# In the second batch the products with v come one step later, each behind the scores of four steps on

## The chip, the cores and the metric

One core of a Trainium2 chip runs the whole program. The metric is the device time of one execution in microseconds, the median of several runs. The engines of the core work in parallel, each through its own queue in order: TensorE (PE, matmuls and the transposes made as matmuls), VectorE (DVE), ScalarE (ACT), GpSimd (POOL) and SyncE (SP), which here issues nearly all DMAs.

## What is computed

Attention in which a query only sees the keys of its own hash bucket, and behind it two MLPs with a gate. Cut to what matters:

```python
q_bits = (einsum('bhsd,dk->bhsk', q, proj) > 0)          # 6 bits, k_bits likewise
mask   = q_bucket[:, :, :, None] == k_bucket[:, :, None, :]
scores = where(mask, q @ k.T / sqrt(64), -1e9)
attn   = exp(scores - max);  attn /= attn.sum(-1) + 1e-9
x = (attn @ v)                                            # 2 batches, 8 heads, 768 x 64
x = x as 1536 tokens x 512
x = gate(x @ w_in,  1.702) @ w_out                        # 512 -> 2048 -> 512
y = gate(x @ w_in2, 1.0)   @ w_out2
```

## The kernel before, in words

**Steps.** A step j is one block of 128 query rows of one head: 16 heads of 6 blocks make 96 steps, 0 to 47 the first batch, 48 to 95 the second. Heads are worked on in pairs. For each step the kernel runs this chain:

- `scores` (L417, L418): four matmuls of 384 columns, two with `aq` and `ak` (q and k split into two parts), two with `BQ` and `BK`, which hold the rows of the mask and the other half of the split. I call the four S j.
- `top` on VectorE (L425) reads the scores from PSUM into `p` and takes the row's extreme; `exps` on ScalarE (L430) is the exponential; `p_high` (L441, ScalarE) rounds to f16 and `p_low` on GpSimd (L445) gives the rest. Both land in `hl`.
- `p_turn` (L451) turns `hl` into `pt` by a DMA transpose from SyncE's queue, one for two steps, j even and j+1. I call such two steps a pair and name it by the even one.
- `av` (L463 to L465): eighteen small matmuls, `pt` times the split v (`VS`). I call them av j. `norm` divides by the row sums when a head is complete.

The mask rows of a pair of heads come from `bits` (L345, matmuls into `psbit`), `signs` (L352, VectorE, `mk`) and `rows` (L360, four DMAs on SyncE's queue: `BK` and `BQ` of the one head, then of the other).

**Beside it.** From step 51 on, the first MLP for the tokens of the first batch is mixed in: `gemm1` (L632, `psh`, twelve matmuls per unit, here h) and `gemm2` (L666, `pso`, six per unit, here o), both with three products of split operands. Its weights come as 64-bit words (`raw`, L139, 512 KB each), are rebuilt on VectorE and ScalarE (L173 to L181), and the split parts are written to DRAM (`spih`, `spil`, `spoh`, `spol`, L186) and read again later (L163). When attention is done, the rest of this MLP and the second one follow; that half is matmuls almost without a break.

**PSUM and buffers.** From step 51 on the scores have one PSUM tile, the products with v one bank, the MLP two, transposes and bits two. `pt` has two buffers.

**What sets the order.** The code is written step by step (L583 to L612): in a turn i it emits av i - LAG, then `top`, the preparation of later heads, `exps`, `p_high`, `p_low`, `p_turn`, some units of the MLP, and in the second batch the scores of i + 1. With LAG = 3, av follows the exponential by three turns. A scheduler then orders each engine's instructions by when it believes them ready and by the priorities in `SOONER`; `issue_after` pins one instruction behind another. So the code's order is not the engine's order.

Of the kernel before, what the change touches and what calls it, by code (L numbers as in the profile page):

```python
# [21 lines left out]
def tile_lsh_attention_two_mlps(  # L22
# [13 lines left out]
    V, A, G, T, SP = nc.vector, nc.scalar, nc.gpsimd, nc.tensor, nc.sync  # L36

    B, H, S, D = q.shape
# [4 lines left out]
    NC = S // P  # L43
    HS = S // 2
    HC = NC // 2
    HEADS = B * H
# [13 lines left out]
    QSCALE = -1.0 / math.sqrt(D)  # L60
    assert math.frexp(QSCALE)[0] == -0.5
    NBUF = 3
    LAG = 3
    TUL = 1
    MORE = {'aq': 1, 'ak': 1, 'p': 1, 'hl': 1, 'pt': 0, 'nk': 1, 'nq': 1, 'nv': 1}
    PTB = 2
# [12 lines left out]

    SOONER = ({'ahead': 100, 'move': 20, 'load_v': 400, 'evict': 200, 'p_high': 200, 'natural': 800, 'p_turn': 35, 'turn': 100, 'p_low': 75, 'top': 35, 'exps': 75, 'bits': 300, 'norm': 35, 'load': 50, 'signs': 20}, {'scores': 200, 'evict': 50, 'norm': 300, 'av': 400, 'natural': 200, 'gate': 50, 'p_turn': 20, 'load_v': 200, 'load': 20, 'sum': 150, 'move': 20, 'p_high': 150, 'rows': 100, 'p_low': 75, 'bits': 100, 'exps': 20}, {'gate': 300, 'sum': 10, 'weights': 50})  # L80
    RATE = (3.4, 2.85)
    SWITCH = HEADS // 2 * NC + LAG + 1
    RING = 3
    RING2 = 6

# [2 lines left out]
    def sooner(task):  # L88
        n = SOONER[stage[0]].get(task, 0)
        return tc.high_priority(offset=n) if n else nullcontext()  # L90
# [161 lines left out]
    def attention(sp, s1, ps_m, ps_v, ahead_of, setup):  # L252
        nat, st = {}, {}
# [12 lines left out]
        N = len(steps)  # L266
# [65 lines left out]
        def place(n):  # L332
            return n % (NBUF + 1) if n < H else (n - H) % NBUF
# [74 lines left out]
        def scores(j):  # L408
            n, c = steps[j]
            aq, ak = st["q", n], st["k", n]  # L410
            bq, bk = BQ[place(n)], BK[place(n)]
            ps = ahead_of["pool"].tile([P, 2, 512], F32, tag="s", name="pss")
            lq = aq.rearrange("p a b -> p (a b)")[:, c * P:(c + 1) * P]
            bq = bq[:, c * P:(c + 1) * P]
            for half in range(2):
                o = ps[:, half, 0:HS]
                T.matmul(o, lhsT=lq, rhs=ak[:, half, :], start=True, stop=False)  # L417
                T.matmul(o, lhsT=bq, rhs=bk[:, half * HS:(half + 1) * HS], start=False, stop=True)  # L418
            st["S", j] = ps[:, :, 0:HS]


# [32 lines left out]
        def av(j):  # L454
            (n, c), g = steps[j], group[j]
            vs, s = st["v", n // 2]
            pt = st.pop(("pt", j))
            if j == g[0]:
                st["av", g] = v_bank("pav")
            o = st["av", g][:, c * (D + 1):(c + 1) * (D + 1)]  # L460
            for i in range(NC):
                hv, lv = vs[:, n % 2, i, 0:D + 1], vs[:, n % 2, i, D + 1:]
                T.matmul(o, lhsT=pt[:, i], rhs=hv, start=(i == 0), stop=False)  # L463
                T.matmul(o[:, 0:D], lhsT=pt[:, i], rhs=lv, start=False, stop=False)  # L464
                T.matmul(o, lhsT=pt[:, NC + i], rhs=hv, start=False, stop=(i == NC - 1))  # L465


        def norm(g):
# [35 lines left out]
        def v_bank(name):  # L504
            j = count["av"] = (count.get("av", -1) + 1) % len(ps_v)
            return ps_v[j].tile([P, 512], F32, tag="av", name=name)
# [31 lines left out]
        def run(fs):  # L538
            for f, *a in fs:
                with sooner(f.__name__):  # L540
                    f(*a)
# [38 lines left out]
            run(ahead(1, s))  # L580


        for lead, first, last in ((2, 0, N // 2), (1, N // 2, N)):  # L583
            def at(f, j):
                if first <= j < last:
                    with sooner(f.__name__):
                        f(j)

            for i in range(first - lead, last + LAG + 1):
                if lead == 2:  # L590
                    at(scores, i + 2)
                at(av, i - LAG)
                at(top, i + lead - 1)
                m = i - LAG
                if first <= m < last and m == group[m][-1]:
                    with sooner("norm"):
                        norm(group[m])
                m = i - 2 * (2 - lead)
                if first <= m < last:
                    pr, s = divmod(m, 2 * NC)  # L600
                    with sooner("ahead"):
                        if pr + 1 < HEADS // 2:
                            run(ahead(pr + 1, s))
                        if s >= 2 * NC - 4 and pr + 2 < HEADS // 2:
                            run(ahead(pr + 2, s - 2 * NC))
                at(exps, i)
                at(p_high, i)
                at(p_low, i)
                at(p_turn, i - TUL)
                yield i  # L610
                if lead == 1:
                    at(scores, i + 1)  # L612
# [108 lines left out]
    with ExitStack() as es:  # L721
# [10 lines left out]
        for i in attention(sp, s1, ps_m, ps_v, ahead_of, lambda: attention_setup(sp, s1, am, ps_m)):  # L732
# [3 lines left out]
            if gen is None and i >= WSTART and i % WEVERY == 0 and W.done < 4:  # L736
                W.step()
            if gen is None and i == SWITCH - 1:
                ps_s.close()
# [57 lines left out]
```

## Time and profile before

| | us |
|---|---|
| median of 3 runs | 806.49 |
| lowest, highest run | 803.45, 806.79 |
| the profiled execution | 809.91 |
| its span in the trace | 807.9 |
| TensorE busy in the span | 740.4 (92%) |
| VectorE, ScalarE, GpSimd busy | 507.3, 422.4, 430.4 |

The span is what the trace covers; the profiled execution's own time is 2.0 us longer. All times of the trace count from the start of its span. The second batch's scores begin at 151 us (S48) and end at 381 us (S95); the last product with v ends at 394 us. A product's wait is shown on its first matmul, in brackets, with what released it.

### The profile page before, as it was taken

To read this page: it belongs to the slowest core of one execution; us is meant where nothing else is said; L and a number is where in the kernel's file an instruction comes from. 1 tells how busy PE (TensorE), PEld (TensorE's weight loads), DVE (VectorE), ACT (ScalarE), POOL (GpSimd) and SP (SyncE) were. 2 spreads that over 40 slices of the span, in tenths; PEclk is the share of its full clock that TensorE was granted. 3 is DMA by queue.
4 is the path that set the end of the run, shared out by engine and by line. 5 is a ranking of instruction groups with operands and counts; after the bars stand their busy time and mean duration, and the time that the engine had idled before them with its cause. 6 is when DMAs were issued, how large, how long until landed. Compare 5 with 4: busy or idle time off the path is not lost.

```text
span 807.9 us, 14034 instructions
## 1 busy us (share of the span) xinstructions
PE 740.4 (92%) x5384; PEld 682.6 (84%) x5384; DVE 507.3 (63%) x932; ACT 422.4 (52%) x721; POOL 430.4 (53%) x345
## 2 busy tenths in 40 slices
PE   6786777678889999899999999979999999999998
PEld 5676666668878898899899999978998899989996
DVE  8987688967689798887332244999545744322222
ACT  6776576586778586676444134445545333311220
POOL 5675567877659666766633133567535334422220
PEclk9898888799999999999999999999999999999999
DMA  5999999999999998885597040333211300000112
GB/s 160 206 191 186 185 204 208 211 247 249 272 225 252 255 227 239 220 188 106 149 387 246 2 157 1 130 108 101 80 52 53 105 1 2 0 1 1 40 40 78
DMA packets 196270, 116.40 MB, mean 144 GB/s; under 512 B 153318, under 2 KB 175846, under 8 KB 196204
## 3 DMA queue, kind: packets, MB, share of 16 engines
q1 hardware_dynamic: 196044, 115.52, 57.5%
q8 instruction: 42, 0.69, 0.3%
q14 instruction: 24, 0.20, 0.1%
q10 hardware_dynamic: 160, 0.00, 0.0%
HBM read 56.63 MB, written 16.78 MB: 91 GB/s over the span
## 4 chain that ended last, share of the span: by engine, by line
PE 66%; DMA 13%; DVE 10%; issue 4%; ACT 3%; POOL 2%; SPq 0%; ACTq 0%; DVEq 0%; POOLq 0%
PE pso L666 29%; PE psh L632 28%; DMA pt<-hl 9%; PE pss L417 2%; PE psbit L345 2%; POOL hl L445 2%; DMA raw<-in_moe_w_in_dram 2%; DVE p L425 2%; PE pss L418 2%; DVE f L176 1%; ACT p L430 1%; PE pav L463 1%; PE pav L464 1%; PE pav L465 1%; DVE f L175 1%
## 5 line engine op out<-in xcount | busy, mean ns | idle before, releaser
L643 POOL TENSOR_TENSOR gl<-g,gh 128x384 fp32r<-128x384 f32 x128 | 136.0, 1064 | 195.7 <-ACT gh L642 183.6
L445 POOL TENSOR_TENSOR hl<-p,hl 128x768 f16<-128x768 f32 x96 | 162.6, 1700 | 71.9 <-ACT hl L441 37.4
L632 PE MATMUL psh<-XH,wih 128*128 128x384 f32 x512 | 174.2, 340 | 1.5 <-DVE part L675 1.0
L632 PE MATMUL psh<-XL,wih 128*128 128x384 f32 x512 | 172.9, 338 | 1.8 <-DVE XL L498 1.8
L632 PE MATMUL psh<-XH,wil 128*128 128x384 f32 x512 | 173.2, 338 | 0.0
L675 DVE SCALAR_TENSOR_TENSOR part<-pso,part 128x384 f32<-128x384 f32 (+1 forms) x124 | 72.6, 591 | 88.8 <-PE pso L666 88.6
L641 DVE TENSOR_TENSOR g<-g,psh 128x384 f32<-128x384 f32 x96 | 52.8, 551 | 117.5 <-ACT g L640 117.5
L430 ACT ACTIVATE p<-p,lo 128x768 f32<-128x768 f32 x96 | 89.7, 936 | 52.7 <-DVE p L425 52.2
L642 ACT CAST gh<-g 128x384 fp32r<-128x384 f32 x128 | 65.5, 513 | 78.7 <-DVE g L641 69.1
L425 DVE TENSOR_SCALAR_CACHE_REDUCE p<-pss 128x768 f32<-128x768 f32 x96 | 90.8, 948 | 15.3 <-PE pss L418 13.3
L632 PEld LDWEIGHTS psh<-XH,wih 128*128 128x128 f32 x512 | 97.5, 190 | 3.1 <-ACT XH L677 1.0
L632 PEld LDWEIGHTS psh<-XL,wih 128*128 128x128 f32 x512 | 97.6, 191 | 2.8 <-DVE XL L498 2.2
L632 PEld LDWEIGHTS psh<-XH,wil 128*128 128x128 f32 x512 | 97.3, 190 | 0.2 <-POOL wil L181 0.2
L640 ACT ACTIVATE g<-psh 128x384 f32<-128x384 f32 x96 | 46.8, 489 | 96.1 <-PE psh L632 95.2
L463 PE MATMUL pav<-VS,pt 128*128 128x65 f16 x576 | 64.4, 198 | 33.9 <-DMA pt<-hl 32.1
L666 PE MATMUL pso<-gh,woh 128*128 128x384 f32 x256 | 87.3, 347 | 6.5 <-ACT gh L642 4.3
L463 PEld LDWEIGHTS <-pt 128*128 128x128 f16 x576 | 54.6, 99 | 44.1 <-DMA pt<-hl 38.9
L666 PE MATMUL pso<-gh,wol 128*128 128x384 f32 x256 | 86.2, 337 | 0.0
L666 PE MATMUL pso<-gl,woh 128*128 128x384 f32 x256 | 86.1, 336 | 0.0
L417 PE MATMUL pss<-ak,aq 128*128 128x384 f32 x192 | 76.0, 397 | 10.8 <-DVE p L425 10.5
L666 PE MATMUL pso<-woh,gh 128*128 128x512 f32 x192 | 74.8, 390 | 0.2 <-ACT gh L642 0.2
L666 PE MATMUL pso<-wol,gh 128*128 128x512 f32 x192 | 75.0, 391 | 0.0
(119 smaller groups left out, 1572.0 us busy)
## 6 DMA issues: line engine op xcount, KB each, us to landing
raw<-in_moe_w_in_dram SPq DMA_DIRECT2D x32, 512.0 KB
raw<-in_moe_w_out_dram SPq DMA_DIRECT2D x32, 512.0 KB
spih<-wih SPq DMA_DIRECT2D x13, 256.0 KB
spil<-wil SPq DMA_DIRECT2D x13, 256.0 KB
spoh<-woh SPq DMA_DIRECT2D x13, 256.0 KB
spol<-wol SPq DMA_DIRECT2D x13, 256.0 KB
wih<-spih SPq DMA_DIRECT2D x13, 256.0 KB
wil<-spil SPq DMA_DIRECT2D x13, 256.0 KB
```

The costliest lines, as they stand in the source:

```text
L417: T.matmul(o, lhsT=lq, rhs=ak[:, half, :], start=True, stop=False)
L425: V.tensor_scalar(p, st.pop(("S", j)), LOW, None, op0=ALU.min, op1=ALU.min, accum_out=lo)
L430: A.activation(p, p, AF.Exp, bias=lo, scale=-1.0)
L445: G.tensor_tensor(out=hl[:, 1], in0=st.pop(("p", j))[0], in1=hl[:, 0], op=ALU.subtract)
L463: T.matmul(o, lhsT=pt[:, i], rhs=hv, start=(i == 0), stop=False)
L632: T.matmul(h, lhsT=a[:, c], rhs=x[t][:, c], start=(n == 0), stop=(n == 3 * NDC - 1))
L640: A.activation(g, h, AF.Sigmoid, scale=beta)
L641: V.tensor_tensor(out=g, in0=g, in1=h, op=ALU.mult)
L642: A.copy(gh[:, f], g)
L643: G.tensor_tensor(out=gl[:, f], in0=g, in1=gh[:, f].bitcast(F32), op=ALU.subtract)
L666: T.matmul(y, lhsT=a, rhs=x, start=(n == 0), stop=(n == 3 * nf - 1))
L675: V.scalar_tensor_tensor(out=acc, in0=y, scalar=scale, in1=acc, op0=ALU.mult, op1=ALU.add)
```

## The change

The number of turns between the exponential and av becomes a pair: three in the first batch, as before, and four in the second. In the second batch av j is also pinned behind the last matmul of S j+4, where there is one.

```diff
-    LAG = 3
+    LAGS = (3, 4)
...
-    SWITCH = HEADS // 2 * NC + LAG + 1
+    SWITCH = HEADS // 2 * NC + LAGS[0] + 1
...
-                T.matmul(o, lhsT=bq, rhs=bk[:, half * HS:(half + 1) * HS], start=False, stop=True)
+                st["did", j] = T.matmul(o, lhsT=bq, rhs=bk[:, half * HS:(half + 1) * HS], start=False, stop=True).ins
...
-            for i in range(NC):
-                hv, lv = vs[:, n % 2, i, 0:D + 1], vs[:, n % 2, i, D + 1:]
-                T.matmul(o, lhsT=pt[:, i], rhs=hv, start=(i == 0), stop=False)
-                T.matmul(o[:, 0:D], lhsT=pt[:, i], rhs=lv, start=False, stop=False)
-                T.matmul(o, lhsT=pt[:, NC + i], rhs=hv, start=False, stop=(i == NC - 1))
+            first = st.get(("did", j + 4)) if j >= N // 2 else None
+            with tc.issue_after(first) if first is not None else nullcontext():
+                for i in range(NC):
+                    hv, lv = vs[:, n % 2, i, 0:D + 1], vs[:, n % 2, i, D + 1:]
+                    T.matmul(o, lhsT=pt[:, i], rhs=hv, start=(i == 0), stop=False)
+                    T.matmul(o[:, 0:D], lhsT=pt[:, i], rhs=lv, start=False, stop=False)
+                    T.matmul(o, lhsT=pt[:, NC + i], rhs=hv, start=False, stop=(i == NC - 1))
...
-        for lead, first, last in ((2, 0, N // 2), (1, N // 2, N)):
+        for lead, first, last, LAG in ((2, 0, N // 2, LAGS[0]), (1, N // 2, N, LAGS[1])):
```

No instruction is added or taken away on any engine. The orders are the same up to S56 and av52 and again once attention is over; between, all five engines are ordered anew. By unit, TensorE's rows from S56 to S60 read before

S56, h, av52, av53, h, S57, h, av54, av55, S58, two matmuls of an h, o, S59, the rest of that h, o, three transposes, S60, av56, av57

and now

S56, h, av52, h, S57, av53, h, S58, av54, S59, av55, three transposes, S60, three transposes, two matmuls of an h, o, av56, S61, av57.

On TensorE, from the last matmul of S57 (first row) to the first of S59 it stood so before; the rows of one unit are cut to its first ones, and `pav` is av54, then av55:

```order
L418 MATMUL pss<-BK_159,BQ_155 128x384
L632 MATMUL psh<-XH_63,wih 128x384
...
L463 LDWEIGHTS pt
L463 MATMUL pav<-VS_170,pt 128x65
...
L418 MATMUL pss<-BK_159,BQ_155 128x384
L632 MATMUL psh<-XH_63,wih 128x384
L632 MATMUL psh<-XL_67,wih 128x384
L666 MATMUL pso<-gh,woh 128x384
...
L417 MATMUL pss<-ak,aq 128x384
```

and so now, with av53, S58's four matmuls and av54 in this order:

```order
L419 MATMUL pss<-BK_159,BQ_155 128x384
L467 LDWEIGHTS pt
L467 MATMUL pav<-VS_170,pt 128x65
...
L636 MATMUL psh<-XH_63,wih 128x384
...
L418 MATMUL pss<-ak,aq 128x384
L419 MATMUL pss<-BK_159,BQ_155 128x384
...
L467 MATMUL pav<-VS_170,pt 128x65
...
L418 MATMUL pss<-ak,aq 128x384
```

The avs of a pair no longer stand together, and between S58 and S59 only av54 is left where an o and two matmuls of an h stood.

On TensorE, the last matmuls of `bits` for the last pair of heads (`psbit`), before: an av and an o follow, and S80 to S83 stand ahead of S84, the first scores that use these mask rows.

```order
L345 MATMUL psbit<-aq,pa_113 52x384
L345 MATMUL psbit<-aq,pb_117 52x384
L463 LDWEIGHTS pt
L463 MATMUL pav<-VS_170,pt 128x65
...
L666 MATMUL pso<-gh,woh 128x384
L666 MATMUL pso<-gl,woh 128x384
```

Now, with an o, the first matmul of S84 (which needs no mask row), an o, an h, and the three other matmuls of S84:

```order
L346 MATMUL psbit<-aq,pb_117 52x384
L670 MATMUL pso<-gh,woh 128x384
...
L418 MATMUL pss<-ak,aq 128x384
L670 MATMUL pso<-gh,woh 128x384
...
L636 MATMUL psh<-XH_63,wih 128x384
...
L419 MATMUL pss<-BK_158,BQ_154 128x384
L418 MATMUL pss<-ak,aq 128x384
L419 MATMUL pss<-BK_158,BQ_154 128x384
L467 LDWEIGHTS pt
```

The matmul that reads the mask rows has moved up to within an o, one matmul, an o and an h of the `psbit` that they come from.

On SyncE's queue, around the mask rows of that pair of heads, before:

```order
L186 DMA spih_3843<-wih 128x512
L360 DMA BK_158<-mk 13x768
L186 DMA spil_3845<-wil 128x512
L360 DMA BQ_154<-mk 13x768
L360 DMA BK_159<-mk 13x768
L360 DMA BQ_155<-mk 13x768
L139 DMA raw<-in_moe_w_out_dram 128x512
L451 DMA_TRANSPOSE pt<-hl 128x24x128
```

and now:

```order
L452 DMA_TRANSPOSE pt<-hl 128x24x128
L187 DMA spil_3827<-wil 128x512
L140 DMA raw<-in_moe_w_out_dram 128x512
L361 DMA BK_158<-mk 13x768
L361 DMA BQ_154<-mk 13x768
L361 DMA BK_159<-mk 13x768
L361 DMA BQ_155<-mk 13x768
L452 DMA_TRANSPOSE pt<-hl 128x24x128
```

The four rows now stand in one piece between the transposes of pairs 80 and 82; before, they stood ahead of the transpose of pair 78.

## Rows read from the trace of the kernel before

**Rows 1.** Busy time of each engine by stretch, over all engines: start and end, length, then busy us (and instructions) of PE, PEld (weight loads), DVE, ACT, POOL, the granted clock of PE as a share, the busy share of the DMA engines, GB/s.

```profile
185.00:400.00 215.00, 201.59 (x1789) 188.43 (x1788) 168.78 (x331) 149.47 (x246) 149.40 (x118) 0.99 0.90 215
400.00:808.00 408.00, 399.44 (x2109) 375.27 (x2107) 188.43 (x292) 146.24 (x285) 156.56 (x137) 1.00 0.24 81
```

**Rows 2.** Whom PE waited for, from 185 to 415 us: us in total, times, longest.

```profile
PE pav L463 <- DMA pt<-hl: 9.4, 8, 2.3
PE pso L666 <- DVE part L675: 1.5, 1, 1.5
PE psh L632 <- DVE part L675: 1.0, 2, 0.7
```

**Rows 3.** The view of rows 1 for two short stretches; the number behind the five engines is the granted clock.

```profile
185.00:205.00 20.00, 17.01 (x155) 15.69 (x154) 14.15 (x27) 13.73 (x24) 13.46 (x12) 1.00 1.11 250
...
272.00:277.00 5.00, 5.00 (x31) 4.84 (x28) 2.54 (x4) 2.29 (x3) 3.74 (x3) 0.66 1.07 290
```

**Rows 4.** PE in order of time: start us, length us, line, operation, in brackets the idle time before it and what ended it. The eight first matmuls of an av that waited for `pt`, of pairs 54, 56, 62, 66, 68, 78, 84 and 92 in this order.

```profile
197.04 0.20 PE L463 MATMUL pav<-VS,pt 128*128 128x65 f16 x1 [1.81 <-DMA pt<-hl]
...
208.34 0.20 PE L463 MATMUL pav<-VS,pt 128*128 128x65 f16 x1 [1.51 <-DMA pt<-hl]
...
237.90 0.20 PE L463 MATMUL pav<-VS,pt 128*128 128x65 f16 x1 [0.39 <-DMA pt<-hl]
...
261.77 0.20 PE L463 MATMUL pav<-VS,pt 128*128 128x65 f16 x1 [0.85 <-DMA pt<-hl]
...
271.69 0.20 PE L463 MATMUL pav<-VS,pt 128*128 128x65 f16 x1 [1.78 <-DMA pt<-hl]
...
325.38 0.20 PE L463 MATMUL pav<-VS,pt 128*128 128x65 f16 x1 [2.29 <-DMA pt<-hl]
...
354.28 0.20 PE L463 MATMUL pav<-VS,pt 128*128 128x65 f16 x1 [0.22 <-DMA pt<-hl]
...
387.05 0.20 PE L463 MATMUL pav<-VS,pt 128*128 128x65 f16 x1 [0.51 <-DMA pt<-hl]
```

**Rows 5.** The same view: the first rows of units that follow each other without a break (an h, S, two h and o between them left out), and an av with the o behind it.

```profile
330.62 0.33 PE L632 MATMUL psh<-XH,wih 128*128 128x384 f32 x1
...
332.70 0.34 PE L417 MATMUL pss<-ak,aq 128*128 128x384 f32 x1
...
335.48 0.33 PE L666 MATMUL pso<-gh,woh 128*128 128x384 f32 x1
...
336.52 0.34 PE L417 MATMUL pss<-ak,aq 128*128 128x384 f32 x1
...
337.22 0.33 PE L666 MATMUL pso<-gh,woh 128*128 128x384 f32 x1
...
250.42 0.20 PE L463 MATMUL pav<-VS,pt 128*128 128x65 f16 x1
...
250.99 0.43 PE L666 MATMUL pso<-gh,woh 128*128 128x384 f32 x1
251.25 0.34 PE L666 MATMUL pso<-gl,woh 128*128 128x384 f32 x1
```

**Rows 6.** SyncE's queue: first all transposes from 185 to 390 us in one row (shortest, median and longest issue in ns, first and last start), then in order of time (start, length of the issue) a weight load and the transposes of pairs 56, 64, 68, 74 and 78.

```profile
L451 SPq DMA_TRANSPOSE pt<-hl x22: 3577/4316/7013, 181.6 to 386.0; - x22
...
198.99 0.38 SPq L139 DMA_DIRECT2D raw<-in_moe_w_in_dram  x1
199.62 6.62 SPq L451 DMA_TRANSPOSE pt<-hl  x1
...
244.07 3.68 SPq L451 DMA_TRANSPOSE pt<-hl  x1
...
265.48 4.16 SPq L451 DMA_TRANSPOSE pt<-hl  x1
...
293.41 4.56 SPq L451 DMA_TRANSPOSE pt<-hl  x1
...
318.38 5.32 SPq L451 DMA_TRANSPOSE pt<-hl  x1
```

**Rows 7.** In order of time: the last matmuls of S65, S69 and S75 on PE, and `p_low` of steps 69 and 79 on POOL.

```profile
235.09 0.34 PE L418 MATMUL pss<-BK,BQ 128*128 128x384 f32 x1
...
254.44 0.34 PE L418 MATMUL pss<-BK,BQ 128*128 128x384 f32 x1
...
287.31 0.34 PE L418 MATMUL pss<-BK,BQ 128*128 128x384 f32 x1
...
259.18 1.66 POOL L445 TENSOR_TENSOR hl<-p,hl 128x768 f16<-128x768 f32 x1
...
314.51 1.65 POOL L445 TENSOR_TENSOR hl<-p,hl 128x768 f16<-128x768 f32 x1
```

**Rows 8.** In order of time, around the mask rows of the last pair of heads: VectorE's read of the scores of step 79, `mk`, and the first `BK` and `BQ` on SyncE's queue; and, from the chain of work that ended last (start, length, what), the smallest load, 64 x 6 numbers, from issue to landing.

```profile
311.63 0.96 DVE L425 TENSOR_SCALAR_CACHE_REDUCE p<-pss 128x768 f32<-128x768 f32 x1 [0.23 <-PE pss L418]
...
313.11 0.66 DVE L352 TENSOR_SCALAR mk<-psbit,thr 52x384 fp32r<-52x384 f32 x1
...
313.80 0.86 SPq L360 DMA_DIRECT2D BK<-mk  x1
...
315.28 0.83 SPq L360 DMA_DIRECT2D BQ<-mk  x1
...
1.31 3.66 DMA pj<-in_proj_dram
```

## The prediction

> **What bounds the kernel now.** I read the busy times by stretch first [rows 1]. From 400 us on TensorE works in 399.4 of 408 us and never sees a product with v; that half can only follow the half ahead of it. From 185 to 400 us, the stretch in which the change moves instructions, TensorE is busy 201.6 of 215 us, far ahead of VectorE (168.8). So TensorE's own work, which the change leaves as it is (7102 matmuls in both orders, and as many instructions on each other engine), is the floor; what can be won or lost is its idle time there, 13.4 us. The view of waits [rows 2] puts 9.4 us of it down to eight waits of a product with v for the transpose that brings its `pt`; the other 4.0 us wait for VectorE and ScalarE. The third view is the granted clock [rows 3]: one dip, at 272 to 277 us, right behind two of those waits (0.85 and 1.78 us [rows 4]). It granted 0.66 on average over 5 us, so 1.7 us were lost (5 x 0.34). What can be won is thus 15.1 us at most, and of the waits that the change aims at 9.4 + 1.7 = 11.1 us, 1.4%.
>
> **Prices.** From starts in one unbroken piece [rows 5]: twelve matmuls of `gemm1` (I call them h) 332.70 - 330.62 = 2.08 us, six of `gemm2` (o) 336.52 - 335.48 = 1.04, the four of one step's scores (S) 337.22 - 336.52 = 0.70, the eighteen of one product (av) 250.99 - 250.42 = 0.57. The matmul behind an av takes 0.26 us to the next start instead of 1.04 / 6 = 0.17, so each place where an av ends before other work costs 0.09 us.
>
> **What is moved, pair by pair.** One transpose serves two steps, m (even) and m+1. It can begin when `p_low` of step m+1 is done, so the av of step m has to wait a certain time behind S of m+1: its need. Its distance is the TensorE work that stands between those two. I counted the distances in both orders with the prices above. Over the 21 pairs from 54 on their mean goes from 12.7 to 14.1 us: the average transpose gets 1.3 us more time. But the order is remade, and some get less. The need comes from the trace: issue of the transpose, its length, and 2.05 us until the av starts (199.62 + 6.62 to 208.34 is 2.1 us, 265.48 + 4.16 to 271.69 is 2.05, 318.38 + 5.32 to 325.38 is 1.7 [rows 4, 6]). I assume the needs stay. Then:
> - Pairs 62, 68, 78, 84, 92 wait today 0.39, 1.78, 2.29, 0.22, 0.51 us [rows 4]. Their distances grow by 1.5 (12.8 to 14.3), 7.6 (13.8 to 21.4), 4.7 (11.5 to 16.3), 2.6 (11.2 to 13.8), 0.7 (11.2 to 12.0). All five waits go: -5.2 us.
> - Pair 66 loses 0.5 us of distance (16.0 to 15.6): its 0.85 us wait grows, +0.5.
> - Pair 74 falls from 12.4 to 11.0 us (av71, h, S76, o, S77, av72 and 73, o, six transposes, o, S78, o). Its need is 293.41 + 4.56 + 2.05 less 287.31 + 0.34, the end of S75 [rows 6, 7]: 12.4 us. A new wait, +1.4.
> - Pair 64 has 14.0 us against a need of 244.07 + 3.68 + 2.05 - 235.43 = 14.4 [rows 6, 7]: +0.4.
> - Pairs 54 and 56: av54 gains 0.8 us of distance, but behind S57 the distance of av56 falls from 9.8 to 7.9 us, because S58, S59 and S60 now follow each other with only single avs between them. Up to av56 TensorE has then done one o less (1.04) and three transposes more (0.2), but S57 stands 0.57 earlier, so it loses 0.3 us if the need stays. That transpose took 6.62 us against a median of 4.3, and a 512 KB weight load was issued just ahead of it [rows 6]; in the new order the load stands behind it. At the median length 2.3 us go. Between -2.0 and +0.3 I take -0.5.
>
> Sum: -5.2 + 0.5 + 1.4 + 0.4 - 0.5 = -3.4 us.
>
> **The other edits.** The dip goes with the waits ahead of it: -1.7 (bounds: 0, or another dip behind a new wait; the wait of 1.81 us at 197 us brought none [rows 3, 4], so I take none). Avs are cut off by other work at 29 places instead of 20: 9 x 0.09 = +0.8. The scores have a single PSUM tile in this stretch, so S(j+1) cannot start before VectorE has read S(j), which takes 0.96 us [rows 8] and some 0.1 to begin. New are three gaps of about that or less: av54 alone between S58 and S59 (0.65 us), av55 and three transposes before S60 (0.86), one o between S76 and S77 (1.04). The first two lie in the time that av56 waits anyway; the third costs 0.1. The upper end, if VectorE is in a weight step of 0.7 us each time, is +2; I take +0.1.
>
> The rows of the mask are what comes late next. S84 reads `BK` and `BQ`, whose rows come from the last `psbit`, by VectorE (`mk`) and two DMAs on SyncE's queue. Before, 21 us of TensorE work stood between; now the last `psbit` is followed by o, one matmul, o and h, 1.04 + 0.17 + 1.04 + 2.08 = 4.3 us, and then the matmul that needs `BQ`. From the start of `mk` the rows take 0.69 us to the first issue, 0.94 to the second [rows 8], then 0.83 + 2.05 (the tail of the transposes) or, by the smallest load in the trace, 3.66 us: 4.5 to 5.3. So 0.2 to 1.0 us; I take +0.6. S72 has 20.9 us from S69; a transpose, three weight spills, a load and the rows themselves pass the queue in that time. I take 0 and keep the rest for the rivals. Behind such a wait stands everything on TensorE, av80 and 81 among it, which the edit forbids to go ahead of S84 and S85; behind a waiting av stand the next scores, h and o. Buffers cost nothing: `pt` has two tiles, and the transpose that takes one again serves steps m+4 and m+5, whose `p_low` comes after S(m+5), when av m+1 is only 0.57 us from its end; the one bank of the products still has an h or two o and a step's scores (2.8 us) between two heads, in which `norm` empties it. The 4.0 us of waits for VectorE and ScalarE stay, and the half behind 400 us too: the weight blocks it reloads were written before, TensorE's order there is unchanged, and on SyncE's queue two loads of the second MLP only move ahead of six reloads that are not needed soon.
>
> **Sum:** -3.4 - 1.7 + 0.8 + 0.1 + 0.6 = -3.6 us. The profiled execution took 809.9 us, 807.9 of them its span; it lies 3.4 us above the median of the three runs, 806.5. It would become 806.3, and the median 802.9. That is 0.45%. About 0.5% (4.0 us, so 802.5 and 810.5) is what a measurement can tell from no change.
>
> **Rivals.** *The needs shrink too.* Spread over the steps, ScalarE, GpSimd and the queue get each pair earlier, and nearly every wait for `pt` goes with the dip: -9.4 - 1.7 + 0.8 = -10.3, 796.2 us. For it: a transpose took between 3.6 and 7.0 us [rows 6]. Against it: nothing in the change touches the amount of work on that queue.
>
> *The queue sets the pace.* SyncE issues the 22 transposes of this stretch at a median of 4.3 us each [rows 6], some 95 of 200 us, with the weight loads, spills and mask rows between them, in order. If attention moves faster, the next transpose stands behind them and comes as late as before; the distance that is won is lost in the need. Then the waits and the dip stay and the breaks cost 0.8: 807.3 us. The rows speak in part for it: the transposes of pairs 68 and 78 were issued 4.6 and 2.2 us after their last `p_low` ended (259.18 + 1.66 to 265.48, 314.51 + 1.65 to 318.38 [rows 6, 7]). (The Trainium skill, "Perfetto Trace Analysis", section What "DMA-bound" means, counts a solid issuing track as a bound of its own. By that rule the result would be this rival's; the trace has that track about half full of transposes, so it agrees in part.)
>
> *The mask rows come late.* At S72 they are issued behind the transpose of pair 68. If that starts 10.7 us behind S69, as today (265.48 against 254.44 + 0.34 [rows 6, 7]), and takes 4.2 to 7.0, then three issues of 0.4 like that of the weight load and the rows (313.80 to 315.28 + 0.83, 2.3 us [rows 6, 8]) and the tail of 2.05 follow: the row lands 20.4 to 23.3 us behind S69, against 20.9 of cover. If the queue is late by another 4.6 us, as it was for pair 68, S72 stalls for up to 7 us, S84 for 1, and a stall of that kind can bring a dip of 1.7. With the gains kept, -3.4 - 1.7 + 0.8 + 7 + 1 + 1.7 = +5.4, so 811.9 us. It decides the sign from about 4 us of lateness on. (The Trainium skill, "TensorE: Matmul & The Clock Gate", Part 1, has idle time drop the clock to half; the one dip in this stretch agrees, two waits of the same size without one don't.)
>
> *The edit does nothing* is out: the order shows 21 pairs with other distances.
>
> **Chances.** My sum, 803 +/- 3 us: 0.48. Needs shrink: 0.22. The queue sets the pace: 0.15. Mask rows late: 0.15. Below 802.5 lie all of the second and some 0.38 of the first: 0.22 + 0.18 = 0.40. Above 810.5 lie 0.14. Between, 0.46. The forecast is the likeliest case, 802.9. The range leaves out the outer part of the second and the fourth: 797 to 811.
>
> **What would show it.** Right: waits for `pt` of 5 to 6 us in 185 to 400 us, none at pairs 68 and 78, new ones at 74 and near 56; no dip in the second batch; the scores of step 95 with five o and two h fewer ahead of them. Wrong: waits of scores for `BQ` of several us at S72 or S84; transposes that start 9 us and more behind their scores; a wait of scores for the VectorE read beyond 2 us in sum; a new dip of the clock; or a changed half behind 400 us, which I cost at nothing.

## The result, and the profile after

The change makes the kernel slower by about 1%; 802.9 us was forecast, with 811 as the upper end of the range.

| | before | after |
|---|---|---|
| median, us | 807.46 (6 runs) | 815.02 (6 runs) |
| lowest, highest | 803.45, 810.45 | 813.98, 820.79 |
| profiled execution; its span | 809.91; 807.9 | 816.1; 814.3 |
| ratio, 95% interval | | 1.0107 [1.0077, 1.0136] |

Three executions among the experiments (1418 and 3999 us, and 1798 of the kernel before) lie far outside and are left out of every median. Single executions of one kernel differ by several us, so one trace is not enough: before and after were profiled once more (among the experiments). The first view is that of the busy times by stretch, of the changed kernel: the two halves that answer to [rows 1], and two short pieces like those of [rows 3]. The number behind the five engines is the granted clock.

```profile
185.00:400.00 215.00, 201.16 (x1755) 184.88 (x1754) 162.53 (x325) 144.91 (x240) 142.86 (x111) 0.98 0.92 221
400.00:814.00 414.00, 405.50 (x2141) 381.38 (x2139) 191.56 (x298) 149.58 (x291) 162.07 (x143) 0.99 0.22 75
204.00:212.00 8.00, 6.80 (x51) 6.34 (x52) 2.86 (x5) 2.88 (x5) 3.12 (x2) 0.57 1.04 284
235.00:239.00 4.00, 3.94 (x28) 3.64 (x29) 0.00 (x0) 1.88 (x3) 2.61 (x2) 0.57 1.17 244
```

TensorE is as busy as before in the first 215 us, but 34 of its instructions fewer are done by then (1755 against 1789 in [rows 1]): the busy time is in part half-clock time, at 1.2 instead of 2.4 GHz. The short pieces show where: 8 x 0.43 = 3.4 us lost at 204 us and 4 x 0.43 = 1.7 at 235 us. Next, whom TensorE waited for in the changed kernel from 185 to 415 us (total us, times, longest), which answers to [rows 2]:

```profile
PE pav L467 <- DMA pt<-hl: 8.8, 5, 3.2
PE pss L419 <- DMA BQ<-mk: 1.7, 2, 0.9
```

and the first matmuls of the five avs that waited (pairs 56, 62, 74, 86, 94), in order of time, for [rows 4]:

```profile
205.20 0.24 PE L467 MATMUL pav<-VS,pt 128*128 128x65 f16 x1 [3.19 <-DMA pt<-hl]
235.06 0.20 PE L467 MATMUL pav<-VS,pt 128*128 128x65 f16 x1 [1.99 <-DMA pt<-hl]
293.44 0.20 PE L467 MATMUL pav<-VS,pt 128*128 128x65 f16 x1 [0.30 <-DMA pt<-hl]
352.73 0.20 PE L467 MATMUL pav<-VS,pt 128*128 128x65 f16 x1 [1.02 <-DMA pt<-hl]
387.13 0.20 PE L467 MATMUL pav<-VS,pt 128*128 128x65 f16 x1 [2.28 <-DMA pt<-hl]
```

Eight waits of 9.4 us became five of 8.8: fewer, but longer. Of the two pieces of half clock the first begins within the wait of 3.19 us, the second 0.3 us behind the one of 1.99.

**Where the time lies.** I take the stretch from the end of S56 to the first h behind the attention: ahead of it both orders are the same, and behind it TensorE needs 404.8 to 405.0 us in all four traces. (S56 itself ends between 185.0 and 189.9 us, although in all the kernels below but those with small spills TensorE's order ahead is the same: much of what single executions differ by arises there.) The stretch of before, before again, after and after again:

```profile
186.90:399.20 212.30, 198.89 (x1772) 185.76 (x1770) 168.14 (x329) 147.26 (x243) 148.42 (x116) 0.99 0.90 216
```

```profile
186.70:395.90 209.20, 197.61 (x1772) 184.29 (x1771) 168.01 (x329) 146.97 (x243) 148.39 (x116) 1.00 0.92 218
```

```profile
186.50:405.60 219.10, 204.61 (x1773) 188.04 (x1771) 165.26 (x329) 146.03 (x243) 148.25 (x116) 0.98 0.93 226
```

```profile
186.80:404.80 218.00, 203.19 (x1772) 187.07 (x1770) 165.84 (x329) 146.38 (x242) 148.25 (x116) 0.98 0.93 228
...
207.00:211.00 4.00, 4.00 (x28) 3.78 (x26) 1.58 (x3) 1.38 (x2) 1.65 (x1) 0.57 1.13 279
326.00:330.50 4.50, 4.25 (x22) 4.06 (x23) 3.19 (x6) 2.37 (x4) 1.66 (x2) 0.62 1.33 199
```

The means are 210.75 us before and 218.55 after, +7.8, about as much as the medians differ (7.6). The two kernels of experiments 12 and 13, whose order in this stretch is that of before, have 211.4 and 208.3 us. The 7.8 us split into three terms. **Idle time**, length less busy time of PE: 13.4 and 11.6 before, 14.5 and 14.8 after, +2.1. **Half clock**: 1.7 us lost [rows 3] and none before, 3.4 + 1.7 and 1.7 + 1.7 after, +3.4. **Cuts**, places where an av ends before other work (the prediction's breaks): in the stretch 47 before and 71 after, counted in the traces; 24 x 0.107 us (measured below) = +2.6. Together 8.1; some 0.3 is counted twice, where a wait lies in half-clock time. The account holds beyond these four: in all fourteen traces of kernels with whole spills, whose stretches are 208.3 to 218.9 us long, the length less idle time, lost clock and 0.107 us for each cut is 190.7 to 193.7 us.

### The profile page after: what moved, and what is told of

Same layout as the page of the kernel before. It is cut to its first block, busy times and chain, and to the rows that moved or that the text cites. A ratio compares the mean times of both kernels' runs of the same rounds, so it can differ in the third digit from the quotient of the medians.

```text
span 814.3 us, 14037 instructions
## 1 busy us (share of the span) xinstructions
PE 745.6 (92%) x5384; PEld 686.6 (84%) x5384; DVE 501.9 (62%) x932; ACT 421.6 (52%) x721; POOL 429.0 (53%) x345
## 4 chain that ended last, share of the span: by engine, by line
PE 67%; DMA 15%; DVE 9%; ACT 5%; issue 3%; POOL 1%; SPq 0%; DVEq 0%; POOLq 0%; ACTq 0%
PE psh L636 29%; PE pso L670 28%; DMA pt<-hl 10%; PE pss L418 2%; DVE p L426 2%; DMA raw<-in_moe_w_out_dram 2%; PE pss L419 2%; PE pav L467 2%; ACT p L431 1%; PE pav L468 1%; DMA raw<-in_moe_w_in_dram 1%; PE pav L469 1%; PE psbit L346 1%; ACT hl L442 1%; DMA nv<-in_v_dram 1%
## 5 line engine op out<-in xcount | busy, mean ns | idle before, releaser
L467 PE MATMUL pav<-VS,pt 128*128 128x65 f16 x576 | 69.4, 202 | 30.7 <-DMA pt<-hl 28.9
```

## Experiments

**Theories.** A: the loss is these three terms, and the first two come from a few pairs whose distance the new order made short; a long wait there draws half clock behind it. Rivals: B, the later lag slows SyncE's queue and makes the mask rows late, whatever TensorE's order is; C, the cuts alone; D, the loss is spread over the stage; E, the new order costs the time, whatever the transposes need. Times stand beside runs of before on the same chip; idle time, half clock and cuts are of the stretch above.

**1. The lag without the hold.**

```diff
-            first = st.get(("did", j + 4)) if j >= N // 2 else None
+            first = None
```

> Lag 4 in the second batch, but the products are not held behind a score. By the order on TensorE a pair's products then stand on average 11.9 us behind its second score (before 12.7, changed kernel 14.0), and 43 of them are cut off by other work (before 47, changed kernel 71). Theory A (cuts at 0.09 us each plus half-clock stretches that follow a long wait): the cuts give nothing, the shorter distance adds 2 to 4 us of waits on pt, and a half-clock stretch follows where such a wait reaches 2 us or more: 808 to 813 us. Theory B (the changed program order of the lag slows SyncE's queue and makes the mask rows late, whatever TensorE's order is): about as slow as the changed kernel, 813 to 816, with waits of S72 and S84 on BQ of 1.7 us in sum. Theory C (cuts alone): 807, as before.

816.16 against 808.13 us, 1.0132 [1.0066, 1.0197], from three runs: no faster than the changed kernel, and over the range of A. The waits, from the view of waits from S56 to the end of the stage:

```profile
PE pav L467 <- DMA pt<-hl: 13.9, 10, 2.7
```

Idle time is 17.4 us, half clock 1.7, cuts 43. B has the time nearly right and the cause wrong: mask rows cost 0.5 us, and the excess is waits on pt. C falls: fewer cuts than before, and slower. Four turns in the code brought the avs earlier on TensorE, not later (11.9 us behind their scores instead of 12.7): the scheduler decides, and it is the hold that keeps them back.

**2. Three steps, held behind the third.**

```diff
-    LAGS = (3, 4)
+    LAGS = (3, 3)
...
-            first = st.get(("did", j + 4)) if j >= N // 2 else None
+            first = st.get(("did", j + 3)) if j >= N // 2 else None
```

> Lag 3 as before, but each product of the second batch is held behind the scores of three steps later. By the order: mean distance 12.0 us, 52 cuts. Theory A: 0.5 us for the cuts and 1 to 4 us for waits on pt, 808 to 813, above 810 only with more half-clock time than the 3.4 us of before. Theory B: as before, 806 to 808.5. Theory C: 808.

813.26, 1.0087 [1.0049, 1.0125]: at the upper edge of A's range, but without the half clock that A asked for above 810; B and C are out. Waits on pt 9.2 us (11 times), on the mask rows 1.9, half clock 1.7, idle 15.3, cuts 52. A lag of three with a hold loses two thirds of what four steps lose (5.1 of 7.6 to 8.1 us).

**3 and 4. The change from step 60 on, and up to 59.** First with the old lag, unheld, up to 59:

```diff
-            first = st.get(("did", j + 4)) if j >= N // 2 else None
+            first = st.get(("did", j + 4)) if j >= 60 else None
...
-                at(av, i - LAG)
+                for late in (4, 3):
+                    if LAG == 3 and late == 3 or LAG == 4 and late == (4 if i - late >= 60 else 3):
+                        at(av, i - late)
```

> The change, but only from step 60 on; products 48 to 59 stay three steps behind and unheld, so that the pair 56/57 stands as before. 66 cuts, mean distance 14.0 us. Theory A: the 3.2 us wait at product 56 and the 6.8 us of half clock behind it go back to about 1.5 us and none; the cuts (1.7 us over before) stay: 809 to 812, 3 to 5 us under the changed kernel. Theory B: 813 to 816. Theory C: 809.2, with the half-clock stretch still in its place behind step 60.

(`norm` moves with the av, here and in the edits like it.) Then the other half, the same code with the conditions `N // 2 <= j < 60` and `< 60`:

> The other half of c_from60: four steps and the hold for products 48 to 59 alone; from 60 on three steps behind and not held. By the order 47 cuts as before, distance 7.9 us at the pair 56/57, mean 12.7. Theory A: the 3.2 us wait at product 56 and the half clock behind it stay, the cuts of the later steps go: 4 to 6 us over before, 811 to 814. Rival D (the loss is spread over the stage and has no place of its own): half of it or less, 807 to 811.

From 60 on: 809.39 against 808.13 us, 1.0022 [0.9993, 1.0050]. Up to 59 alone: 814.98 against 807.73, 1.0082 [1.0055, 1.0109], with as many cuts as before. The two medians lie 1.3 and 7.3 us over their runs of before, 8.5 in sum, and the whole change 7.6 and 8.1: nearly all of the loss comes with the edit to products 48 to 59, and D falls. From 60 on lies in A's range, and as near to C's 809.2, which experiment 1 has ruled out otherwise; B's 813 to 816 is missed. Up to 59 lies 1 us over A's range. (The trace of the kernel up to 59 is of an execution of 812.0 us, 3 below its median; its stretch, 214.5 us, shows about half of its loss.) The waits of the kernel from 60 on:

```profile
PE pav L467 <- DMA pt<-hl: 3.1, 2, 1.6
PE pss L419 <- DMA BQ<-mk: 2.5, 2, 2.2
PE pso L675 <- DVE part L684: 2.1, 1, 2.1
```

and, of the kernel up to 59, av56, the clock behind it, and the waits on pt:

```profile
206.85 0.24 PE L467 MATMUL pav<-VS,pt 128*128 128x65 f16 x1 [3.56 <-DMA pt<-hl]
...
206.00:211.00 5.00, 4.15 (x42) 3.85 (x43) 1.67 (x4) 2.02 (x3) 0.87 (x2) 0.66 1.03 331
...
PE pav L467 <- DMA pt<-hl: 8.3, 6, 3.6
```

From 60 on the change does what it says: the 5 to 6 us of waits on pt behind step 60 go. But 19 cuts more (2.0 us), the wait for the mask rows, and two pieces of half clock, behind the waits of 2.1 and 2.2 us for `part` and for the rows, take it back. Up to 59 it brings the wait at av56 and its half clock, and idle time at later steps whose order shifted with it (1.54 us at av62, 1.87 at S71, 1.07 at av86).

**5. One unit put back ahead of av56.** The o that stood there before must come first again (`all_o` lists the matmuls of `gemm2` in the code's order).

```diff
+            unit = all_o[6 * 6 - 1] if j == 56 else None
-            with tc.issue_after(first) if first is not None else nullcontext():
+            with tc.issue_after(first) if first is not None else nullcontext(), tc.issue_after(unit) if unit is not None else nullcontext():
```

> The changed kernel with one edge more: product 56 also waits for the gemm2 unit that stood ahead of it before. The order gives the pair a distance of 11.4 us (changed kernel 7.9) and 58 cuts (71). Theory A: the wait at 56 goes from 3.2 to at most 1 us with no half clock behind it, and the fewer cuts give 1.2: 808 to 811. Rival D: 813 to 816.

813.44 against 807.73, 1.0072 [1.0048, 1.0095]: 2.4 us better than the changed kernel on the same chip (815.81, experiment 6), where A expected 5 to 8 and D none; the two intervals overlap. Waits from S56 on:

```profile
PE pav L469 <- DMA pt<-hl: 5.8, 5, 2.1
PE pss L419 <- DVE p L427: 2.5, 3, 1.4
PE pss L420 <- DMA BQ<-mk: 2.4, 1, 2.4
```

The wait at 56 is gone and no half clock follows there; but the scheduler ordered all that comes behind anew, and a wait of 2.4 us for the mask rows of S84 has half clock behind it. A is right about the wait and wrong that the loss hangs on it alone: idle time is 14.9 us as in the changed kernel, made of other waits; what fell is the half clock (to 1.7 us) and 13 cuts.

**6. Both kernels once more.** Unchanged, for second traces.

> The changed kernel once more, for a second trace. Theory A (the long waits on pt at products 56 and 62 come from the order on TensorE and draw the half clock behind them): the same two waits, 3.2 and 2.0 us within 0.5, and half clock within 1 us behind each; 813 to 817. Rival (the half-clock stretches fall by chance): the waits are there again, the half clock stands elsewhere or is missing, and the time within the stretch moves with it by 1.7 us for each 3.4 us of it.

> The kernel before once more, for a second trace. If waits and half clock of the first trace are typical: 13 us of waits between the end of step 56's scores and the first unit of the next stage, half clock at 272.5 again, span 806 to 809. If the half clock falls by chance: the same waits on pt within 1 us each, half clock elsewhere or none, span 803 to 806.

After again: 815.81, 1.0098 [1.0076, 1.0119]. The waits on pt are nearly the same (2.80 us at av56, 1.55 at av62, 2.27 at av94), the one of S84 for the mask rows is 1.83 instead of 0.89. The half clock behind av56 is there for 3.4 us instead of 6.8, behind av62 it is missing, and behind S84 it is new. Before again: 806.67 us, span 804.5, seven waits on pt of 8.2 us in sum, no half clock at all. So the waits repeat from one execution to the next, mostly within 0.5 us, as A has it. Where the half clock stands does not repeat, as the rival has it, but it is not blind: it left a wait that had become shorter (av62) and came to one that had become longer (S84). Between waits of about the same length chance decides: of before's waits of 1.78, 1.81 and 2.29 us the shortest alone was followed.

**7. Pairs kept together, and held longer.** Both products of a pair behind the fourth score after its second step.

```diff
-    LAGS = (3, 4)
+    LAGS = (3, 5)
...
-            first = st.get(("did", j + 4)) if j >= N // 2 else None
+            first = st.get(("did", (j | 1) + 4)) if j >= N // 2 else None
...
-                at(av, i - LAG)
+                for m in (i - 3,) if LAG == 3 else (i - 5, i - 4) if i % 2 else ():
+                    at(av, m)
```

> Both products of a pair issued together behind the scores of five and four steps later (behind the fourth score after the pair's second step). Mean distance 16.2 us, 55 cuts. Theory A: cuts +0.7; if the needs stay near 14 us (pairs of the changed kernel: 10.9 to 17.7) the waits on pt fall from 8.8 to 2 to 4 us and no long wait is left for a half-clock stretch to follow: 800 to 805. If the needs rise as much as the distances, the waits stay at 7 to 9 us and it is 806 to 812. Theory B: 813 to 816. Theory C: 808.2.

808.65, 1.0026 [0.9996, 1.0056]: not the gain; A's 800 to 805 is missed though its condition held. The waits on pt did fall to 2.5 us, the needs stayed (14.2 us on average), and no half clock is left:

```profile
PE pss L418 <- DVE p L426: 3.2, 2, 2.2
PE pss L419 <- DMA BQ<-mk: 2.9, 2, 1.5
PE pav L467 <- DMA pt<-hl: 2.5, 3, 1.4
PE psh L637 <- ACT wih L181: 2.0, 2, 1.5
```

The time went to waits of the scores for VectorE's read, for the mask rows and for split weights, which in the trace of before took 0.3, 0 and 0.5 us.

**8 and 9. The mask rows from ScalarE, and all of it from step 60 on.** First:

```diff
-                SP.dma_start(out=dst[place(n)][0:R].bitcast(F32),
+                (A if pr >= 6 else SP).dma_start(out=dst[place(n)][0:R].bitcast(F32),
```

> e_pairs with the mask rows of steps 72 and 84 sent from ScalarE instead of SyncE. In e_pairs the scores of these steps waited 2.9 us on the rows, which stood in SyncE's queue behind a transpose of 4.6 us. If the queue is the cause: no wait on BQ, 804 to 807. If the time is only passed on to pt, p or the weights: 807 to 809.

808.80 against 807.73, 1.0008 [0.9992, 1.0024]: passed on. The waits, then around S72 `mk` on VectorE and the first row on ScalarE's queue:

```profile
PE pss L418 <- DVE p L426: 5.4, 3, 2.7
PE pss L419 <- DMA BQ<-mk: 2.1, 2, 1.2
...
258.19 0.66 DVE L353 TENSOR_SCALAR mk<-psbit,thr 52x384 fp32r<-52x384 f32 x1
258.89 1.38 ACTq L361 DMA_DIRECT2D BK<-mk  x1
```

The first row goes out 0.04 us behind `mk`, and S72 waits still: in this order `mk` itself is late. In the changed kernel it was not so. There the rows of S72 lay ready for 4.3 us, behind a transpose of 6.1 us and three transfers on SyncE's queue:

```profile
258.83 0.66 DVE L353 TENSOR_SCALAR mk<-psbit,thr 52x384 fp32r<-52x384 f32 x1
...
263.78 0.86 SPq L361 DMA_DIRECT2D BK<-mk  x1
```

At S84 they went out 0.5 us behind `mk` (0.8 in the second trace). So B has a share, but no more than the waits for mask rows, 1.7 and 2.4 us of 7.8. Then the same with the products up to 59 as before the change (conditions as in 3):

> h_pairs_rows_act with the products up to 59 as before the change: pairs together behind the fourth score from step 60 on, mask rows of steps 72 and 84 from ScalarE. By the order 47 cuts as before and a mean distance of 15.9 us. Theory A: the waits on pt behind step 60 go (3.7 to 5 us of the first trace of before), nothing is added in cuts: 801 to 805, faster than before by 0.2 to 0.8%. If the waits only move to p, the mask rows and the weights, as in e_pairs: 806 to 809.

808.37 against 807.41, 1.0019 [1.0000, 1.0038], with 47 cuts as before and 3.2 us more distance by the order:

```profile
PE pav L467 <- DMA pt<-hl: 5.7, 4, 1.9
PE pso L677 <- DVE part L686: 1.9, 1, 1.9
PE pss L419 <- DMA BQ<-mk: 1.3, 2, 1.1
```

Idle time is 12.6 us, between the two traces of before: A's 801 to 805 is missed, the rival's 806 to 809 holds. No version beats the kernel before.

**10 and 11. Smaller spills, before and after.** A quarter of each spill is written, and read back four times; the second half then computes with wrong weights.

```diff
-                    SP.dma_start(out=t.bitcast(F32), in_=d)
+                    SP.dma_start(out=t.bitcast(F32), in_=d.to_broadcast([P, NDC, P]))
...
-                    d = spill.tile([P, NDC, P], F32, name=f"sp{kind}{part}{block[1]}")
-                    SP.dma_start(out=d, in_=t.bitcast(F32))
+                    d = spill.tile([P, 1, P], F32, name=f"sp{kind}{part}{block[1]}")
+                    SP.dma_start(out=d, in_=t[:, 0:1].bitcast(F32))
```

> The kernel before with the spills of the split weights cut to a quarter (one of four column blocks is written to memory and read back for all four, so the second half of the program computes with wrong weights). Less traffic beside the transposes: the mean from a pair's second score to its landing, 13.5 us in the trace of before, falls by 0.5 to 1.5 us, the waits on pt by 3 to 6 us of 9.4: 800 to 804. If the traffic of the spills is not what stretches the transposes: 806 to 809.

> The changed kernel with the same cut of the spills. 76 cuts against 61 in m_before_small. Theory A: with shorter needs the waits on pt go in both, no long wait is left for half clock, and what remains of the 8 us between the two is the cuts, 15 by 0.09 = 1.4 us: 801 to 806, 1 to 3 over m_before_small. Rival E (the new order itself costs the time, whatever the needs are): 6 to 9 us over m_before_small.

Before with small spills: 821.15, 1.0174 [1.0142, 1.0205], from four runs. After with small spills: 810.16, 1.0022 [1.0000, 1.0044]. Both expectations fall, and so does the sign: here the change is faster, by 11 us. The scheduler, which sees smaller transfers, ordered both kernels anew from S50 on. The stretch and the first waits of the one before,

```profile
187.60:408.10 220.50, 200.78 (x1755) 188.24 (x1752) 166.23 (x328) 145.76 (x240) 146.98 (x115) 0.96 0.74 160
...
PE pav L463 <- DMA pt<-hl: 10.7, 6, 3.5
PE psh L632 <- ACT wih L180: 3.5, 1, 3.5
```

and of the one after:

```profile
187.60:394.40 206.80, 196.29 (x1754) 179.97 (x1751) 165.87 (x328) 144.04 (x239) 146.01 (x114) 1.00 0.86 190
...
PE pav L467 <- DMA pt<-hl: 3.4, 4, 1.6
PE pss L418 <- DVE p L426: 2.6, 2, 2.4
```

The issue of a transpose takes 4.3 us on average instead of 4.6 to 4.7, and yet the kernel before got four waits of 2.5 to 3.5 us, each with half clock at it (9.3 us lost), against no half clock after, for all its 76 cuts. As both orders are new, the two runs don't show what shorter transposes alone would do. Of E this leaves: the order costs the time, but not this lag's order as such. What the change is worth turns on where a few pairs land in a given order.

**12 and 13. The price of a cut.** In the second layer of the MLP, where TensorE hardly waits, n f16 products of av's shape ahead of each of 64 h, with n = 1 and n = 18:

```diff
+                for _ in range(n if layer == 1 else 0):
+                    T.matmul(ps[:, 0:D + 1], lhsT=warm, rhs=warm[:, 0:D + 1], start=True, stop=True)
```

> The price of a cut by itself: the kernel before, with one f16 product of av's shape (128x65, of a constant tile, overwritten by the unit that follows) ahead of each of the 64 gemm1 units of the second layer, where TensorE waits for nothing. If a cut costs the 0.09 us that the prediction took: 64 x (0.0315 + 0.09) = +7.8 us in the time from the first unit behind the attention to the end (404.8 us in both traces of before). If it costs nothing beyond the product's own slot: +2.0 us.

> The same with 18 f16 products, as many as a whole av has, ahead of each of the 64 units. With 0.09 us for the cut: 64 x (18 x 0.0315 + 0.09) = +42.0 us from the first unit behind the attention to the end; with nothing: +36.3. The difference to q_switch1 over 17 x 64 gives the slot of one product and so separates it from the cut.

The first h behind the attention and the last matmul of the program, of before again, n = 1 and n = 18, with one such place of n = 1:

```profile
395.88 0.41 PE L632 MATMUL psh<-XH,wih 128*128 128x384 f32 x1 [0.74 <-DVE part L675]
...
800.28 0.39 PE L666 MATMUL pso<-woh,gl 128*128 128x512 f32 x1
```

```profile
396.36 0.41 PE L636 MATMUL psh<-XH,wih 128*128 128x384 f32 x1 [0.74 <-DVE part L679]
...
560.17 0.20 PE L633 MATMUL psh<-warm 128*128 128x65 f16 x1
560.21 0.42 PE L636 MATMUL psh<-XH,wih 128*128 128x384 f32 x1
560.47 0.34 PE L636 MATMUL psh<-XL,wih 128*128 128x384 f32 x1
...
809.61 0.39 PE L670 MATMUL pso<-woh,gl 128*128 128x512 f32 x1
```

```profile
398.24 0.41 PE L636 MATMUL psh<-XH,wih 128*128 128x384 f32 x1 [0.74 <-DVE part L679]
...
845.28 0.39 PE L670 MATMUL pso<-woh,gl 128*128 128x512 f32 x1
```

404.40, 413.25 and 447.04 us, from one execution each, each with one piece of half clock of the same 3.4 us: +8.85 and +42.64, per place 0.138 and 0.666. A product takes (0.666 - 0.138) / 17 = 0.031 us, and what is left is the cut: 0.107 us. The matmul behind the f16 product has 0.26 us to the next start, as in [rows 5].

## Why the prediction was wrong

It had the sign wrong. By its terms, in the order of its sum (measured: after less before, each the mean of two traces):

| term | predicted | measured |
|---|---|---|
| waits of avs on pt | -3.4 | -0.65 (9.4, 8.2 to 8.8, 7.5) |
| half clock | -1.7 | +3.4 |
| cuts | +0.8 | +2.6 |
| mask rows | +0.6 | +2.05 (0, 0 to 1.7, 2.4) |
| one PSUM tile for scores, other waits | +0.1 | +0.7 |

The largest miss is the half clock (5.1 us), then the waits on pt (2.75), the cuts (1.8) and the mask rows (1.45).

- **Waits on pt.** By pair, as means of two traces: 68, 78, 84 and 92 lost 3.9 us where 4.8 was forecast. At 64, 66 and 74, where 2.3 was to be added, 0.8 went. Pairs 54 and 56 together changed by -0.2 (forecast -0.5). What failed is three pairs: 62 gained 1.4 us where its 0.39 was to go, and 86 and 94, which were on no list, gained 0.8 and 2.3.
- **The needs stay** is the step that failed at 86 and 94. On average it nearly held (over 21 pairs, by issue, its length and 2.05 us, or by the av's start where it waited: 13.6 us in both traces of before, 14.2 and 14.1 after), but at 86 the need rose by some 2 us, and at 94, where at most 10.6 us were needed in before again, it was 12.6. The 2.05 us from the end of the issue to the av came from three pairs; the same trace had 3.4 and 3.5 us at its waits of pairs 62 and 92. Only pairs that already waited, or lost distance, were looked at; a pair with 0.5 us to spare needed looking at too.
- **Other waits as cover.** At 62 the need was about 16 us in the first traces of both kernels. Before, waits of 2.1 us for other things stood between S63 and av62 and were cover for the transpose as good as any matmul; after, there were none, and TensorE arrived 1.4 us earlier. In the second pair of traces the need rose by 1.1 instead. The step counted work alone, and TensorE's work there grew by 0.6 us, not by 1.5.
- **Pairs 54 and 56** came near by luck. The count of one o less and three transposes more leaves out ten matmuls of an h, which the new order puts behind av56. TensorE's busy time from the end of S56 to av56, before and after:

```profile
187.00:208.30 21.30, 16.84 (x152) 15.19 (x150) 16.02 (x30) 14.85 (x26) 14.21 (x12) 1.00 1.08 269
```

```profile
186.70:205.20 18.50, 14.32 (x139) 12.87 (x138) 16.34 (x30) 15.68 (x27) 16.35 (x13) 0.98 1.01 230
```

  It fell by 2.5 us, so with S57 0.6 earlier the pairs lost 1.9 and not 0.3 us if the need stayed. The need fell too, by 2.2 us (from S57's last matmul to av56 15.5 us before, 13.3 now; 1.7 in the second traces), close to the 2.3 that the text held possible, and the two all but cancel. S57's last matmul, before and after:

```profile
192.81 0.34 PE L418 MATMUL pss<-BK,BQ 128*128 128x384 f32 x1
```

```profile
191.89 0.34 PE L419 MATMUL pss<-BK,BQ 128*128 128x384 f32 x1
```

  Av56 starts at 208.34 [rows 4] and 205.20. But av54's wait of 1.81 us and av56's of 1.51 became a single one of 3.19 (2.80 in the second trace): no more idle time, but in one piece, and both times half clock followed it. The forecast added waits up and never asked how they lie.

- **Half clock.** "I take none" rested on one wait that brought none. By its own sum some 2.8 us of waits stayed at pairs 54 and 56 alone, and the dip of before stood behind one of 1.78; so the forecast had no ground for taking the clock as mended. This term alone is 5 us of the error.
- **Cuts**: the stretch has 47 and 71, not 20 and 29. The forecast's count fits the places where other work cuts an av in its middle (20 and 30 in the traces); the ends of avs that no longer stand beside their pair's other one (27 and 41) are missing. The price, 0.09, was near the measured 0.107.
- **Mask rows**: the mechanism at S84 was right (0.9 and 1.8 us for 0.6); S72, taken as 0, added 0.8 and 0.5. The rival built on it put its price at 8 us; its cause, rows held on SyncE's queue behind a transpose, is what the trace shows at S72, at a tenth of its size. (The 0.94 us from the first row's issue to the second's are not in [rows 8], which has 1.48 with a spill between; the changed kernel has 0.92.)
- **The rivals.** The needs did not shrink. The queue did not set the pace: transposes start 0.6 to 0.7 us behind their `p_low` on average in all four traces, more than half of them within 0.05. No rival had waits move to other pairs.
- **Right**: the half behind 400 us took as long as before, and the waits for `p` stayed small. (The 7102 matmuls that the text counts are 5384 in every trace of the two kernels; nothing rests on it.)

What stays open: why the needs of pairs 86 and 94 rose, and why the edit up to 59 leaves more idle time at later pairs than the one from 60 on. The orders behind step 60 differ, and one forced by hand, with the early piece of the one kernel and the later piece of the other, was not tried.

## What to carry to other kernels

Where a scheduler remakes the order, an edit is worth what it does at the few shortest pairs, not in the mean: list every pair's slack in the new order, with the longest tail that the trace shows, counting today's other waits as cover that may vanish with it. And ask whether short waits run together into a long one. A wait that is hidden shows the next one behind it; in a stage with VectorE, the mask rows and the weights close behind, 3 us more of distance gave nothing. And price interleaving: 24 cuts more cost 2.6 us without a single wait.

## What the runs showed of the hardware

- **Half clock follows single waits, the longer the likelier.** In the stretch from S56 to the end of attention the sixteen traces have 17 pieces of half clock. Each begins within a wait of TensorE or at most 1.8 us behind one, the shortest of these waits 1.78 us. Of waits over 2.6 us 6 of 8 were followed, of those from 1.8 to 2.6 us 10 of 23, from 1.5 to 1.8 one of 21, from 1.0 to 1.5 none of 33. (The Trainium skill, "TensorE: Matmul & The Clock Gate", section HAM oscillation — how this bites in real kernels, tells of waits for DMA that throw the clock back; the traces agree, here from 1.78 us of wait on, and waits for other engines do it as well: 3.49 us for split weights, 2.13 for `part`.)
- **An f16 product between f32 matmuls** costs 0.031 us of its own and 0.107 for the change, 0.09 of it seen at the matmul behind it (0.26 us to the next start instead of 0.17).
- **A transpose's landing** is no fixed time behind its issue: at the 25 avs that waited for one from pair 54 on, in the two traces of each kernel, the av starts 1.5 to 3.6 us behind the end of the issue. Of the last transpose in the changed kernel the issue is over at 383.6 us and av94 starts at 387.1, 3.5 us behind; the second trace has 3.5 as well.
